# One plan orders all engines of a fused chunk-selecting attention and squared-relu feed-forward

## The chip, the core and the metric

The kernel runs on 1 core of a Trainium2 chip: TensorE (PE, with its weight loads as PEld), VectorE (DVE), ScalarE (ACT), GpSimd (POOL) and SyncE (SP), each with a queue of its own that it works off in order, joined by semaphores. The metric is the device time of one execution in microseconds.

## The reference

```python
def _attn_ref(q, k, v):                  # B, H, S, D = 4, 8, 768, 64
    chunk, nc, top_k, scale = 32, S // 32, 6, 1.0 / np.sqrt(D)
    k_chunks = k.reshape(B, H, nc, chunk, D)
    k_min, k_max = np.min(k_chunks, axis=3), np.max(k_chunks, axis=3)
    ub = np.sum(np.maximum(q[:, :, :, None, :] * k_min[:, :, None, :, :],
                           q[:, :, :, None, :] * k_max[:, :, None, :, :]), axis=-1)
    causal = pos[:, None] // chunk >= np.arange(nc)[None, :]
    ub = np.where(causal, ub, -1000000000.0)
    top_chunks = np.argsort(ub, axis=-1)[..., -top_k:]
    scores = scale * np.matmul(q, k.transpose(0, 1, 3, 2))
    mask = sel & (pos[:, None] >= pos[None, :])      # sel: the key's chunk is in top_chunks
    attn = softmax(np.where(mask, scores, -1000000000.0))
    return np.matmul(attn, v)

x = attn_out.transpose(0, 2, 1, 3).reshape(B * S, H * D)     # 3072 x 512
h = np.maximum(x @ w_in, 0.0)                                # w_in 512 x 2048
out = h * h @ w_out                                          # w_out 2048 x 512
```

## The kernel before

All matmuls are in bfloat16. A batch has 8 heads, taken as 4 pairs, so there are 16 pairs (`p`). A head's 768 positions are 6 tiles of 128. In the first tile of a batch every allowed chunk is among the six best, so it needs no selection: the first tiles of all batches are done ahead (`first_transpose`, `first_scores`, `first_values`), and the other 5 tiles pair by pair.

`stage_a(p)` prepares a pair: it turns the keys on PE (`kT`) and copies them to `kqs` for each head (ACT for p < 3, else DVE), reduces each chunk to its maximum and minimum (`kr`, then `kbds`), turns the queries (`qT`), splits them into positive and negative part (`qp`, `qm`) and copies them to `qss` (ACT), forms the bounds `ub` on PE, masks them (`ubm`), takes each row's 8 largest (`m8`), marks the chunks below the sixth (`selb`), turns these marks on PE (`sT`) and copies them into the last 24 rows of `qss` (DVE). The matching 24 rows of `kqs` hold -32768 for the key's chunk, so that the scores' matmul itself masks what is not selected.

`stage_b(p)` works on 5 banks of 512 score columns for each of 2 heads (`BANKS`): two matmuls into a PSUM bank `ps`, an exp on ACT into `e`, a mask of the diagonal blocks (`causal`: a product with `tri` on DVE for p < 6, an affine select on POOL after that), and four value matmuls of 65 columns into `av`, whose last column is the sum. `normalise` divides on DVE into `x`.

The feed-forward (`ffn_units`) runs on the first tiles of all batches (512 rows, `x_first`) and then on each batch's other 640 rows: `turn` transposes x, `up` makes 128 hidden units for 512 or 320 rows (4 matmuls into `ph`, relu on ACT into `ht`, square on DVE into `h2`), `down` sums 16 hidden blocks into 128 rows of output in four parts, copies them on ACT and stores them from SP's queue.

The order: what PE does in the main part is written by hand. `run_ffn()` lets feed-forward units of the batch before into `stage_b` at a steady rate, after every masked bank; `values` runs `LAG` = 3 banks behind the scores; `beside()` runs one of the four pieces of the next pair's `stage_a` at the banks in `PIECES`; `KEEP` units are left for the end of a batch. The other engines are ordered by the framework's scheduler in that part; in the part of the first tiles all engines go in written order. Loads are issued from POOL's queue in the order of the text: first tiles of k, q, v of batches 0 and 1, then of 2 and 3, w_in's first quarter, then pair by pair the rest of batch 0 with the weights' other quarters between, then batches 1 to 3 tile by tile. POOL must also make the masks, and at most 8 of its loads are under way.

PSUM's 8 banks are `tp` 1 (turned keys and queries), `ps` 3 (scores, also `ub` and `sT`), `av` 2, `ff` 2 (feed-forward); the last batch's `up` uses `ps`.

```python
    with tc.manual_schedule(engines={nc.tensor.engine}):
        ffn.extend(ffn_units(x_first, [S * b for b in range(B)], [(0, 512)]))
...
        run(B)
        aside.append((0, stage_a(0)))
        for n in (2, 2, 2, 2):
            beside()
            run(n)
```

Of the kernel before, what the change touches and what calls it, by code (L numbers as in the profile page):

```python
# [9 lines left out]
F32 = mybir.dt.float32  # L10
# [4 lines left out]
PSUM = bass.MemoryType.PSUM  # L15


@with_exitstack
def kernel(
# [30 lines left out]
    LAG = 3  # L50
# [6 lines left out]
    epool = ctx.enter_context(tc.tile_pool(name="epool", bufs=LAG + 3))  # L57
# [6 lines left out]


    first = {nm: consts.tile([128, B, H, D], BF16, tag=nm + "0", name=nm + "0")
             for nm in "kq"}
    vfirst = consts.tile([128, B, H, VW], BF16, tag="v0", name="v0")
    SRC = {"k": k, "q": q, "v": v}
    nat = {}  # L70

    def load_first(nm, b0, b1):
        dst = vfirst[:, b0:b1, :, 0:D] if nm == "v" else first[nm][:, b0:b1]
        nc.gpsimd.dma_start(
            out=dst.rearrange("p b h d -> p (b h) d"),
            in_=SRC[nm][b0:b1, :, 0:128].rearrange("b h p d -> p (b h) d"))

    def rest(nm, b):
        if (nm, b) not in nat:
            nat[nm, b] = ld.tile([128, NS, H, VW if nm == "v" else D], BF16,  # L80
                                 tag=nm + "n", name=nm + "n")
            if nm == "v":
                nc.gpsimd.memset(
                    nat[nm, b][:, :, :, D:D + 1].rearrange(
                        "p j h o -> p (j h) o"), 1.0)
        return nat[nm, b]

    def load_tile(nm, b, j):
        nc.gpsimd.dma_start(
            out=rest(nm, b)[:, j - 1, :, 0:D],  # L90
            in_=SRC[nm][b, :, 128 * j:128 * (j + 1)].rearrange("h p d -> p h d"))

    def load_pair(nm, b, hp):
        for h in (2 * hp, 2 * hp + 1):
            nc.gpsimd.dma_start(  # L95
                out=rest(nm, b)[:, :, h, 0:D],
                in_=SRC[nm][b, h, 128:].rearrange("(j p) d -> p j d", p=128))

    def key_tile(nm, b, hp, j):
        t = first[nm][:, b] if j == 0 else nat[nm, b][:, j - 1]  # L100
        return t[:, 2 * hp:2 * hp + 2].rearrange("p h d -> p (h d)")

    def value_tile(b, h, j):
        t = vfirst[:, b] if j == 0 else nat["v", b][:, j - 1]
        return t[:, h, 0:D + 1]

    w_in_sb = consts.tile([128, NKI, d_ff], BF16, tag="w_in_sb")
    w_out_sb = consts.tile([128, NFI, d_model], BF16, tag="w_out_sb")

    def load_w_in(f0, f1):  # L110
        cols = slice(128 * f0, 128 * f1)
        nc.gpsimd.dma_start(
            out=w_in_sb[:, :, cols],
            in_=moe_w_in[:, cols].rearrange("(ki p) f -> p ki f", p=128))

    def load_w_out(f0, f1):
        nc.gpsimd.dma_start(
            out=w_out_sb[:, f0:f1],
            in_=moe_w_out[128 * f0:128 * f1].rearrange("(fi p) d -> p fi d", p=128))

    load_first("k", 0, 2)
    ident = consts.tile([128, 128], BF16, tag="ident")
    make_identity(nc, ident)
    load_first("q", 0, 2)
    load_first("v", 0, 2)
    load_first("k", 2, 4)
    load_first("q", 2, 4)
    load_first("v", 2, 4)
    load_w_in(0, 4)
    tri = consts.tile([128, 128], BF16, tag="tri")  # L130
    nc.gpsimd.memset(tri, 1.0)
    nc.gpsimd.affine_select(
        out=tri, in_=tri, compare_op=ALU.is_ge, fill=0.0, base=0,
        channel_multiplier=-1, pattern=[[1, 128]])


# [24 lines left out]
    for i in range(2 * NSET):  # L161
        kq_rows(i)
# [371 lines left out]
```

## Time and profile before

| | |
|---|---|
| time, median of 2 runs | 295.37 us (295.32 to 295.42) |
| profiled execution: its own time | 295.43 us |
| its span, first to last instruction | 293.70 us |
| granted TensorE clock, mean | 0.999 |
| busy PE, PEld | 264.5 us (90%), 172.5 us (59%) |
| busy DVE, ACT, POOL | 190.7 (65%), 195.4 (67%), 102.8 us (35%) |
| DMA, moved in all | 20.61 MB |

The times of the rows are microseconds from the start of the span. Busy time is the union of the recorded spans of an engine's instructions; matmuls overlap, and their recorded ends are modelled. An idle time in brackets names what ended it.

### The profile page before, as it was taken

The page shows a single profiled execution, that of the slowest core. Times are in us where ns is not written, and L with a number is a line of the kernel's source. Part 1 is how long each engine was busy: PE and PEld are TensorE (multiplying, and loading weights), DVE is VectorE, ACT ScalarE, POOL GpSimd, SP SyncE. Part 2 cuts the span into 40 slices and gives each one's busy share as a digit, 9 for nine tenths or more (in the row PEclk, how much of TensorE's full clock was granted, in tenths as well). Part 3 has the DMA queues.
Part 4 walks back from the last instruction along what each step waited for, and adds up shares of the span by engine and source line. Part 5 has one row for each costly group of instructions (what it writes and reads, how often), then busy time and mean ns, then how long its engine had stood idle before and what let it go on. Part 6 is the DMA issues. An engine that isn't in the chain of part 4 may idle for free.

```text
span 293.7 us, 6676 instructions
## 1 busy us (share of the span) xinstructions
PE 264.5 (90%) x2528; PEld 172.5 (59%) x2528; DVE 190.7 (65%) x645; ACT 195.4 (67%) x376; POOL 102.8 (35%) x180
## 2 busy tenths in 40 slices
PE   0578878799899989999998999999989999899994
PEld 0365345565567767555676766557767655577442
DVE  0486777988888989574887895658878720465100
ACT  2223599968768898675788885748798755188211
POOL 8978993999961002121121222111111211000000
PEclk9999999999999999999999999999999999999999
DMA  9999999999999000111100001110000011100011
GB/s 66 168 187 171 160 175 189 155 156 179 175 181 91 1 2 1 38 38 71 38 1 2 3 0 38 71 38 37 2 4 0 2 71 39 71 2 0 36 74 71
DMA packets 82893, 20.61 MB, mean 70 GB/s; under 512 B 75525, under 2 KB 79789, under 8 KB 82861
## 3 DMA queue, kind: packets, MB, share of 16 engines
q0 software_dynamic: 79152, 13.64, 59.6%
q1 hardware_dynamic: 3708, 6.55, 6.0%
q8 instruction: 20, 0.33, 0.4%
q14 instruction: 13, 0.10, 0.1%
HBM read 27.26 MB, written 6.29 MB: 114 GB/s over the span
## 4 chain that ended last, share of the span: by engine, by line
PE 63%; DVE 12%; POOL 8%; ACT 8%; DMA 5%; issue 2%; ACTq 0%; POOLq 0%
PE py L357 25%; PE ph L342 20%; PE ps L427 8%; DVE kr L261 5%; PE av L410 5%; DMA vn<-in_v_dram 3%; ACT ht L347 3%; DVE kqc L258 3%; ACT qsc L281 2%; DMA w_out_sb<-in_moe_w_out_dram 2%; POOL qn L95 2%; POOL kn L95 2%; ACT e L434 2%; PE sT L305 2%; DVE h L350 1%
## 5 line engine op out<-in xcount | busy, mean ns | idle before, releaser
L434 ACT ACTIVATE e<-ps 128x512 bf16<-128x512 f32 x160 | 93.9, 598 | 32.2 <-PE ps L427 29.9
L342 PE MATMUL ph<-xT,w_in_sb 128*128 128x320 bf16 (+1 forms) x576 | 97.8, 312 | 3.0 <-ACT ht L347 2.8
L357 PE MATMUL py<-w_out_sb,h 128*128 128x512 bf16 x384 | 94.7, 378 | 0.0
L347 ACT ACTIVATE ht<-ph 128x320 bf16<-128x320 f32 (+1 forms) x144 | 64.9, 455 | 18.4 <-PE ph L342 10.9
L342 PEld LDWEIGHTS <-w_in_sb 128*128 128x128 bf16 x576 | 56.2, 98 | 29.9 <-issue 7.6
L192 POOL TENSOR_SCALAR_AFFINE_SELECT e<-e 128x128 bf16<-128x128 bf16 x80 | 26.9, 336 | 131.4 <-ACT e L434 131.4
L427 PE MATMUL ps<-qsc,kqc 88*128 88x128 bf16 (+1 forms) x320 | 60.6, 272 | 0.2 <-DVE qsc L309 0.2
L350 DVE TENSOR_TENSOR h<-ht 128x320 bf16<-128x320 bf16 (+1 forms) x144 | 47.0, 333 | 19.2 <-ACT ht L347 18.5
L357 PEld LDWEIGHTS <-h 128*128 128x128 bf16 x384 | 36.9, 97 | 32.5
L410 PEld LDWEIGHTS <-e 128*128 128x128 bf16 x640 | 40.8, 98 | 24.1
L410 PE MATMUL av<-vn,e 128*128 128x65 bf16 x480 | 40.6, 193 | 0.0
L261 DVE TENSOR_REDUCE kr<-kT 128x24 bf16<-128x768 bf16 x32 | 29.2, 953 | 4.5 <-ACT kqc L256 4.4
L362 ACT COPY ob<-py 128x512 f32<-128x512 f32 x24 | 14.1, 586 | 24.2 <-PE py L357 24.1
L281 ACT COPY qsc<-qT 64x640 bf16<-64x640 bf16 x32 | 22.0, 687 | 1.1 <-DVE qm L279 0.5
L427 PEld LDWEIGHTS <-kqc 88*128 88x128 bf16 x320 | 21.7, 98 | 0.8 <-issue 0.2
L258 DVE COPY kqc<-kT 64x768 bf16<-64x768 bf16 x26 | 14.4, 554 | 10.6 <-PE kT L251 10.2
L200 DVE TENSOR_TENSOR x<-av,rc 128x320 bf16<-128x320 f32 (+1 forms) x40 | 19.0, 475 | 0.8
L309 DVE COPY qsc<-sT 24x640 bf16<-24x640 bf16 x32 | 15.5, 483 | 4.9 <-PE sT L305 4.0
L199 DVE RECIPROCAL rc<-av 128x5 f32<-128x5 f32 (+1 forms) x40 | 7.5, 187 | 16.7 <-PE av L410 16.7
L189 DVE TENSOR_TENSOR e<-e,tri 128x128 bf16<-128x128 bf16 (+2 forms) x56 | 14.4, 258 | 3.6 <-ACT e L434 2.0
L296 DVE MAX8 m<-ubm 128x8 f32<-128x24 f32 x160 | 15.4, 172 | 0.5
L410 PE MATMUL av<-v,e 128*128 128x65 bf16 x160 | 15.4, 194 | 0.0
(61 smaller groups left out, 234.4 us busy)
## 6 DMA issues: line engine op xcount, KB each, us to landing
out_dram<-ob SPq DMA_DIRECT2D x24, 256.0 KB, 2.7
w_in_sb<-in_moe_w_in_dram POOLq DMA_DIRECT2D x4, 512.0 KB, 8.0
w_out_sb<-in_moe_w_out_dram POOLq DMA_DIRECT2D x4, 512.0 KB, 8.6
kn<-in_k_dram POOLq DMA_DIRECT2D x15, 128.0 KB, 6.7
qn<-in_q_dram POOLq DMA_DIRECT2D x15, 128.0 KB, 6.8
vn<-in_v_dram POOLq DMA_DIRECT2D x15, 128.0 KB, 6.3
kn<-in_k_dram POOLq DMA_DIRECT2D x8, 80.0 KB, 5.9
qn<-in_q_dram POOLq DMA_DIRECT2D x8, 80.0 KB, 5.2
```

The costliest lines, as they stand in the source:

```text
L192: nc.gpsimd.affine_select(out=e, in_=e, compare_op=ALU.is_ge, fill=0.0, base=0, channel_multiplier=-1, pattern=[[0, n], [1, 128]])
L200: nc.vector.tensor_mul(x, av[:, :, 0:D], rc[:, 0:n].unsqueeze(2).to_broadcast([128, n, D]))
L258: nc.vector.tensor_copy(kqs[0:D, s, hh], pt[D * hh:D * hh + D])
L261: nc.vector.tensor_reduce(kr[:, mm], pt.rearrange("d (c j) -> d c j", j=CH), axis=AX.X, op=op)
L281: nc.scalar.copy(qss[0:D, s, hh], pt[D * hh:D * hh + D])
L342: nc.tensor.matmul(ph, lhsT=w_in_sb[:, ki, 128 * f:128 * (f + 1)], rhs=xT[:, ki, c0:c1], start=(ki == 0), stop=(ki == NKI - 1))
L347: nc.scalar.activation(ht, ph, ACT.Relu)
L350: nc.vector.tensor_mul(h2[f][:, c0:c1], ht, ht)
L357: nc.tensor.matmul(py, lhsT=h2[f][:, 128 * t:128 * (t + 1)], rhs=w_out_sb[:, f, :], start=(f == 0), stop=(f == NFI - 1))
L410: nc.tensor.matmul(av[:, t - 1], lhsT=e[:, 128 * c:128 * (c + 1)], rhs=value_tile(b, 2 * hp + hh, j), start=(i == 0 and c == 0), stop=(i = ...
L427: nc.tensor.matmul(ps[:, 128 * c:128 * (c + nt)], lhsT=kqs[:, s, hh, 128 * j:128 * (j + 1)], rhs=qss[:, s, hh, 128 * (t0 - 1):128 * (t0 - ...
L434: nc.scalar.activation(e, ps, ACT.Exp, scale=scale)
```

## The change

A class `Plan` takes every step of the kernel as an operation: the engines that may do it with a rough duration in us for each, a due time in half steps (20 to a pair, a pair's preparation due 30 earlier), the operations that it needs, the buffers that it uses, and for a load the packets. `order()` simulates the engines: it always takes the operation that can start first, and among those of the same engine that can start within 0.06 us the one due first. Loads keep their listed order, 8 under way at most; buffers come free when the last user is done, plus a hand-over; reads of one PSUM tile by two engines don't overlap; PE's durations are doubled up to 14 us. The operations are then written out in the order of their planned starts, and all engines run in that order.

Other things that go with it: key copies, query copies, selection copies, x copies, relus and output copies go to DVE or ACT, diagonal masks to DVE or POOL, whichever the plan finds free. The first tiles' causal mask is added on PE (a product of `ident` with `ahead`, 512 columns for each of 8 banks) instead of multiplied on DVE. `sT` is turned in 3 matmuls (two tiles each) instead of 5 and copied in 4 pieces instead of 2. The keys and queries of the first tiles are turned into separate banks. Loads: w_in's first quarter and pair 0's k and q come before the first tiles of batches 2 and 3. Eight matmuls of 512 columns on a constant run at the very start. The first quarter of the first feed-forward's ups runs in two halves of 256 columns.

```diff
--- before.py
+++ after.py
+    HAND_OVER = {"PE": 0.22, "ACT": 0.10, "DVE": 0.10, "POOL": 0.12, "SP": 0.1}
+    BUSY = 0.06
+    WAIT = 0.06
+    WARM = 14.0
+    NEVER = 1e9
...
+        while ready:
+            found = []
+            for op in ready:
+                if op.packets and op is not self.loads[len(landed)]:
+                    continue
+                at = 0.0
+                new = {}
+                for t in op.tiles:
+                    if not t.held:
+                        new[t.tag] = new.get(t.tag, 0) + 1
+                for tag, n in new.items():
+                    at = max(at, sorted(slots[tag])[n - 1]
+                             if n <= len(slots[tag]) else self.NEVER)
+                if at == self.NEVER:
+                    continue
+                if op.packets and len(landed) >= 8:
+                    at = max(at, landed[-8])
+                for engine, cost in op.where.items():
+                    st = max(at, free[engine])
+                    for n in op.needs:
+                        same = n.engine == engine and not n.packets
+                        lag = (0.0 if engine == "PE" else self.BUSY) if same                             else self.HAND_OVER[n.engine]
+                        st = max(st, n.end + lag)
+                    for t in op.tiles:
+                        if t.psum:
+                            for e, end in t.last.items():
+                                if e != engine and "PE" not in (e, engine):
+                                    st = max(st, end + self.HAND_OVER[e])
+                    found.append((st, op, engine, cost))
+            assert found, "nothing can start"
+            first = min(found, key=lambda f: f[0])
+            st, op, engine, cost = min(
+                (f for f in found if f[2] == first[2] and f[0] <= first[0] + self.WAIT),
+                key=lambda f: (f[1].due, f[0]))
+            ready.remove(op)
+            if engine == "PE" and st < self.WARM:
+                cost *= 2
+            op.engine, op.start, op.end = engine, st, st + cost
+            free[engine] = op.end
+            if op.packets:
+                queue = max(queue, op.end + 1.3) + op.packets * 0.00098
+                op.end = queue + 0.35
+                landed.append(op.end)
+            for t in op.tiles:
+                if not t.held:
+                    t.held = True
+                    slots[t.tag].remove(min(slots[t.tag]))
+                t.last[engine] = max(t.last.get(engine, 0.0), op.end)
+                t.left -= 1
+                if not t.left:
+                    slots[t.tag].append(
+                        max(u.end + self.HAND_OVER[u.engine] for u in t.users))
+            for n in waiting.get(op, ()):
+                count[n] -= 1
+                if not count[n]:
+                    ready.append(n)
+            done.append(op)
...
+    def write(self):
+        for op in self.order():
+            for t in op.tiles:
+                if t.tile is None:
+                    t.tile = t.make()
+            op.fn(op.engine)
...
+    plan = Plan({"tp": 1, "ps": 3, "av": 2, "ff": 2, "e": 6, "h2": NFI + 6, "ht": 3,
+                 "ob": 3, "kn": B - 1, "qn": B - 1, "vn": B - 1, "x": 2, "xT": 2,
+                 "kr": 2, "qp": 2, "qm": 2, "ubm": 2, "m8": 2, "rc": 2})
...
+    load_first("k", 0, -998)
+    made["ident"] = plan.op({"POOL": 0.75}, -997, lambda _: make_identity(nc, ident))
+    load_first("q", 0, -996)
+    load_first("v", 0, -995)
+    made["ahead"] = plan.op({"POOL": 0.55}, -994, make_ahead)
+    made["tri"] = plan.op({"DVE": 0.15}, -900, lambda _: nc.vector.tensor_single_scalar(
+        tri, ahead, 0.0, op=ALU.is_ge), [made["ahead"]])
+    made["rows", 0] = plan.op({"ACT": 0.84}, -999, lambda _: kq_rows(0),
+                              [made["ident"]])
+    for i in range(1, 2 * NSET):
+        made["rows", i] = plan.op({"SP": 0.8}, -999 + i, lambda _, i=i: kq_rows(i),
+                                  [made["rows", 0]])
+
+    load_w_in(0, 4, -990)
+    made["ubmask"] = plan.op({"POOL": 1.45}, -971, make_ubmask)
+    ones(0, -980)
+    load_pair("k", 0, 0, -989)
+    load_pair("q", 0, 0, -988)
+    for nm in "kqv":
+        load_first(nm, 2, -987)
+    load_w_in(4, 8, -986)
+    load_pair("v", 0, 0, -985)
...
+                load_tile(nm, b, j, 20 * NP * b - 70 + 5 * i + j)
...
+    made["warm"] = plan.op({"PE": 1.7}, -999, lambda _: warm_up(8), [made["vector"]])
...
+            for hh in range(2):
+                nc.tensor.matmul(ps[hh].tile, lhsT=ident,
+                                 rhs=ahead.unsqueeze(1).to_broadcast(
+                                     [128, NP, 128]),
+                                 start=True, stop=False, skip_group_check=True)
...
+        t0 = HALVES * p - LEAD
+        before = scored.get(p - NSET, [])
...
+        def turn_selection(_):
+            for i in range(0, NT, 2):
+                transpose(sT[:, i // 2], selbs[:, s, i:i + 2])
...
+        kc = [op({"DVE": 0.50, "ACT": 0.75}, t0 + 3 + hh + late, lambda e, hh=hh: copy(
+            e, kqs[0:D, s, hh], kT[D * hh:D * hh + D]),
+            [t] + before, [kT]) for hh in range(2)]
...
+    HALVES = 20
+    LEAD = 30
...
-    PIECES = (0, 3, 5, 8)
-    KEEP = 4
...
+                sc = plan.op({"PE": 0.225}, due, scores, prepared[p, hh], [ps])
+                scored[p].append(sc)
+                done = plan.op({"ACT": 0.54}, due + 0.5, lambda _, e=e, ps=ps:
+                               nc.scalar.activation(e.tile, ps.tile, ACT.Exp,
+                                                    scale=scale), [sc], [ps, e])
                 if diagonal:
                     d0, d1 = diagonal
-                    causal(e[:, 128 * d0:128 * d1].rearrange(
-                        "p (n j) -> p n j", j=128), d1 - d0, p < 6)
-                run_ffn()
-                behind.append(lambda p=p, hh=hh, i=i, e=e, x=x:
-                              values(p, hh, i, e, x))
-                if len(behind) > LAG:
-                    behind.pop(0)()
-                if len(BANKS) * hh + i in PIECES:
-                    beside()
-
-
+                    n = d1 - d0
+                    done = plan.op(
+                        {"DVE": 0.10 + 0.07 * n, "POOL": 0.2 + 0.13 * n}, due + 1.5,
+                        lambda en, e=e, d0=d0, d1=d1: causal(
+                            en, e[:, 128 * d0:128 * d1].rearrange(
+                                "p (n j) -> p n j", j=128), d1 - d0),
+                        [done, made["tri"]], [e])
+                prev = plan.op({"PE": 0.125}, due + 5, values,
+                               [done, prev, made["ones", b]] + loads_of("v", b, hp),
+                               [e, av, nat["v", b]])
...
+            op = plan.op({"ACT": 0.06 + w / 960, "DVE": 0.06 + w / 960}, at[0] + 0.5,
+                         relu, [op], [ph, ht])
+            squared.setdefault(f, []).append((c0, c1, plan.op(
+                {"DVE": 0.02 + w / 1200}, at[0] + 2, lambda _: nc.vector.tensor_mul(
+                    h2[f][:, c0:c1], ht.tile, ht.tile), [op], [ht, h2[f]])))
...
+            op = plan.op({"ACT": 0.54, "DVE": 0.53}, at[0] + 1,
+                         lambda e: copy(e, ob.tile, py.tile), [op], [py, ob])
...
+        turn, up, down = ffn(
+            x, lambda t, b=b: x_done[b, 1], [S * b + 128 * t for t in range(1, NT)],
+            None, HALVES * NP * (b + 1) + 10, 2.2, ("ps", "ps") if last else ("ff", "ff"))
...
+        plan.write()
```

## Rows read from the trace of the kernel before

**Rows 1.** Groups by shape, whole run: line, engine, tiles, shapes, count | busy us, mean ns | idle.

```profile
L357 PE MATMUL py<-w_out_sb,h 128*128 128x512 bf16 x384 | 94.7, 378 | 0.0
...
L342 PE MATMUL ph<-xT,w_in_sb 128*128 128x320 bf16 x512 | 79.9, 298 | 3.0 <-ACT ht L347 2.8
...
L347 ACT ACTIVATE ht<-ph 128x320 bf16<-128x320 f32 x128 | 55.4, 437 | 13.2 <-PE ph L342 6.1 <-DVE h L350 1.0 <-PE ps L427 0.3
L427 PE MATMUL ps<-qsc,kqc 88*128 88x384 bf16 x128 | 41.3, 323 | 0.0
...
L410 PE MATMUL av<-vn,e 128*128 128x65 bf16 x480 | 40.6, 193 | 0.0
...
L342 PE MATMUL ph<-xT,w_in_sb 128*128 128x512 bf16 x64 | 17.9, 418 | 0.0
L200 DVE TENSOR_TENSOR x<-av,rc 128x320 bf16<-128x320 f32 x32 | 15.6, 488 | 0.5
L309 DVE COPY qsc<-sT 24x640 bf16<-24x640 bf16 x32 | 15.5, 483 | 4.9 <-PE sT L305 4.0
```

**Rows 2.** The chain that ended last, at its end: start us, us, what.

```profile
255.25 17.52 PE ph L342 x128
272.77 17.28 PE py L357 x80
```

**Rows 3.** Windows: length, each engine's busy us (instructions), granted clock, DMA share, GB/s.

```profile
0.00:26.00 26.00, 13.28 (x120) 9.60 (x121) 12.45 (x39) 6.71 (x11) 21.62 (x35) 1.00 1.71 143
0.00:37.00 37.00, 22.90 (x171) 13.98 (x172) 20.19 (x65) 13.18 (x21) 32.27 (x48) 1.00 1.73 151
37.00:90.00 53.00, 46.62 (x518) 30.52 (x517) 44.31 (x157) 42.94 (x75) 43.65 (x53) 1.00 2.06 172
90.00:254.00 164.00, 159.25 (x1626) 107.12 (x1625) 114.27 (x388) 122.36 (x244) 26.86 (x80) 1.00 0.10 26
254.00:290.00 36.00, 35.71 (x221) 20.86 (x218) 11.93 (x36) 16.34 (x36) 0.00 (x0) 1.00 0.10 37
```

The engines stand in the order PE, PEld, DVE, ACT, POOL.

**Rows 4.** Timeline of PE, 6 to 38 us: start, us, what, [idle before].

```profile
6.12 0.61 PE L213 MATMUL T<-ident,k 128*128 128x128 bf16 x4 [6.12 <-DMA k<-in_k_dram]
...
24.77 0.74 PE L251 MATMUL kT<-ident,kn 128*128 128x128 bf16 x5
25.39 3.57 PE L342 MATMUL ph<-xT,w_in_sb 128*128 128x512 bf16 x8
...
31.71 1.89 PE L342 MATMUL ph<-xT,w_in_sb 128*128 128x512 bf16 x8
...
37.00 0.38 PE L427 MATMUL ps<-qsc,kqc 88*128 88x256 bf16 x2
```

**Rows 5.** Timeline of POOL's queue, 16 to 85 us.

```profile
16.96 0.86 POOL L95 DMA_DIRECT2D vn<-in_v_dram  x1 [0.34 <-DMA v<-in_v_dram]
...
19.49 1.73 POOL L95 DMA_DIRECT2D kn<-in_k_dram  x2 [1.67 <-DMA w_in_sb<-in_moe_w_in_dram]
...
51.99 1.75 POOL L89 DMA_DIRECT2D qn<-in_q_dram  x2 [1.66 <-DMA w_out_sb<-in_moe_w_out_dram]
...
84.14 0.27 POOL L83 MEMSET vn<- 128x40 bf16 x1 [2.32 <-PE av L410]
```

**Rows 6.** Waits, whole run: engine and line, released by: us, times, longest us.

```profile
PE sT L305 <- DVE selb L297: 3.1, 5, 1.4
...
PE ph L342 <- ACT ht L347: 2.8, 5, 0.9
```

**Rows 7.** Groups by shape, 37 to 90 us, of DVE and of ACT.

```profile
L189 DVE TENSOR_TENSOR e<-e,tri 128x128 bf16<-128x128 bf16 x28 | 6.0, 215 | 2.0 <-ACT e L434 1.8
...
L281 ACT COPY qsc<-qT 64x640 bf16<-64x640 bf16 x10 | 6.9, 687 | 0.3 <-DVE qm L279 0.2
```

**Rows 8.** Line L350, 255 to 290 us and 90 to 254 us: ns min/median/max, first and last start.

```profile
L350 DVE TENSOR_TENSOR h<-ht x32: 324/326/326, 256.3 to 273.3; 128x320 bf16<-128x320 bf16 x32
...
L350 DVE TENSOR_TENSOR h<-ht x95: 278/321/542, 91.3 to 230.6; 128x320 bf16<-128x320 bf16 x95
```

More of the change, by code (lines that the diff above doesn't have):

```diff
@@ L15, with __init__, __getitem__ @@
 PSUM = bass.MemoryType.PSUM
+class Buffer:
+    def __init__(self, tag, make, psum=False):
+        self.tag, self.make, self.psum = tag, make, psum
+        self.users = []
+        self.left = 0
+        self.tile = None
+        self.held = False
+        self.last = {}
+    def __getitem__(self, key):
+        return self.tile[key]
+class Op:
+    def __init__(self, where, due, fn, needs, tiles, packets):
+        self.where, self.due, self.fn = where, due, fn
+        self.needs, self.tiles, self.packets = needs, tiles, packets
+        self.engine = None
+        self.start = self.end = None
@@ L78, in rest @@
[L78 to L119, printed above, removed]
@@ L130, with transpose @@
+    def transpose(dst, src):
+        nc.tensor.matmul(dst, lhsT=src, rhs=ident, is_transpose=True,
+                         start=True, stop=True)
+    ident = consts.tile([128, 128], BF16, tag="ident")
+    ahead = consts.tile([128, 128], BF16, tag="ahead")
     tri = consts.tile([128, 128], BF16, tag="tri")
[L131 to L134, printed above, removed]
+    warm = consts.tile([128, 128], BF16, tag="warm")
@@ L234, in first_values, with load @@
-    def first_values(b):
-        es = e_first.pop(b)
-        for hh in range(2):
-            av = psav.tile([128, NP, D + 1], F32, tag="av", name="av0")
+    made = {}
+    made["vector"] = plan.op({"DVE": 1.1}, -999, vector_constants)
+    SRC = {"k": k, "q": q, "v": v}
+    nat = {}
+    loaded = {}
+    order = []
+    def load(key, fn, due, packets, tiles=(), cost=0.88):
+        op = plan.op({"POOL": cost}, due, fn, tiles=tiles, packets=packets)
+        loaded.setdefault(key, []).append(op)
@@ new lines, in ones, with go, load_tile @@
+    def ones(b, due):
+        def go(engine):
+            e = nc.vector if engine == "DVE" else nc.gpsimd
+            e.memset(nat["v", b].tile[:, :, :, D:D + 1].rearrange(
+                "p j h o -> p (j h) o"), 1.0)
+        made["ones", b] = plan.op({"DVE": 0.12, "POOL": 0.3}, due, go,
+                                  tiles=[nat["v", b]])
+    def load_tile(nm, b, j, due):
+        load((nm, b), lambda _: nc.gpsimd.dma_start(
+            out=nat[nm, b].tile[:, j - 1, :, 0:D],
+            in_=SRC[nm][b, :, 128 * j:128 * (j + 1)].rearrange("h p d -> p h d")),
+            due, 1024, [nat[nm, b]])
@@ new lines, with warm_up, first_transposes, turn @@
+    t_first = {}
+    x_done = {}
+    def warm_up(n):
+        wt = psav.tile([128, 4, 128], F32, tag="av", name="wt")
+        for _ in range(n):
+            nc.tensor.matmul(wt, lhsT=warm,
+                             rhs=warm.unsqueeze(1).to_broadcast([128, 4, 128]),
+                             start=True, stop=True)
+    made["warm"] = plan.op({"PE": 1.7}, -999, lambda _: warm_up(8), [made["vector"]])
+    def first_transposes(nm, b, tag, due):
+        pt = buffer(tag, [128, NP, 128], name="T0")
+        t = t_first[nm, b] = buffer("h2", [128, NP, 128], name="t0")
+        def turn(_):
+            for hp in range(NP):
+                transpose(pt[:, hp], key_tile(nm, b, hp, 0))
+        op = plan.op({"PE": 0.23}, due, turn,
+                     loaded[nm, b, "first"] + [made["ident"]], [pt])
+        t.op = plan.op({"DVE": 0.36, "ACT": 0.53}, due + 0.5,
+                       lambda e: copy(e, t.tile, pt.tile), [op], [pt, t])
```

664 lines of the change are left out of this document (373 added, 291 removed).

## The prediction

> **What bounds the kernel now.** I first read the counts by shape of the whole run, to know how much streaming TensorE cannot avoid, and then the windows, to see where it did not stream. The page's busy time of PE (264.5 us, 90%) is no measure of it: a matmul of 65 columns shows 193 ns and one of 512 shows 378 [rows 1], and these overlap. What one costs in a row of others is read from the tail, where nothing else runs: 128 matmuls of 320 columns in 17.52 us, 137 ns each, and 80 of 512 in 17.28 us, 216 ns each [rows 2]. That is 0.42 ns a column; for the other widths I put about 2.5 ns on top (128 columns 56 ns, 384 162 ns, and as estimates at the same pace 30 ns for 65 columns and 26 ns for 48).
>
> With the counts [rows 1]: down 384 x 0.216 = 82.9; up 512 x 0.137 + 64 x 0.216 = 84.0; scores, 160 banks of 512 columns in two pieces each (128 of them as 384 + 128, in the row, 32 as 256 + 256) x 0.218 = 34.9; values 640 x 0.030 = 19.2 (480 in the row, 160 read the first tiles); 416 transposes and small scores of 128 columns x 0.056 = 23.3; 192 short ones 5. Together about 248.5 us of streaming, in a span of 293.7. TensorE bounds the kernel, and 45.2 us are lost to it.
>
> The same prices, counted inside each window [rows 3], say where. Up to 26 only 6.2 us are streamed, up to 37 it is 13.6: lost 23.4. From 37 to 90, 43.9: lost 9.1. From 90 to 254, 155.8: lost 8.2. From 254 to 290, 35.2: lost 0.8. After the last matmul (272.77 + 17.28 = 290.05 [rows 2]) 3.65 remain for the last copy and store. These make the 45.2. So the places to look at are the first 37 us and then the attention of batch 0, up to about 85; the long steady part streams 95% of its time.
>
> The start is bound by arrivals and by the written order. The first keys land at 6.12, yet the keys of pair 0 are turned at 24.77 and its first scores run at 37.00 [rows 4]. Its data were there sooner: v of batches 2 and 3, sixth in the queue, lands by 16.96, w_in's first quarter by 19.49, as the waits of the POOL queue show [rows 5]; pair 0's keys are next, about 20.8. Then they wait because run(B) is written ahead of stage_a(0): the turns of x_first of all four batches come first on PE. Also to be seen there: eight matmuls of 512 columns take 3.57 us at 25.39 (446 ns each, half pace) and 1.89 at 31.71 (full pace) [rows 4], while the granted clock reads 1.00, the 2.4 GHz level, all along [rows 3]. The pace tells more here than that column.
>
> From 37 to 90 DVE is busy 44.3 and ACT 42.9 of 53 us [rows 3], and PE waits for single steps made there (sT for selb 3.1, an up for the relu before it 2.8 [rows 6]). The last values of batch 0 end about 84, when POOL may fill the next vn [rows 5].
>
> **The change, part by part.** *Loads and start.* Three of the six first loads (batches 2 and 3) move behind w_in's first quarter and pair 0's k and q. Five such loads landed between 6.12 and 16.96 [rows 4, 5], 2.17 us each, so three fewer bring pair 0's data 6.5 us sooner: keys at 14.3, queries about 15.7. No matmul of batches 2 and 3 stands before the turn any more. From the turn to the scores it took 37.00 - 24.77 = 12.2 us [rows 4] with relus and squares between; I take 11.5, and scores start at 26. What waits behind the moved loads is batches 2 and 3 (about 21.5 for 17) and w_in's second quarter, some 2 us later; their matmuls can fill after 26. By 26 are streamed: first attention 4.5, a quarter of the first ups 3.5, pair 0's turns; some 8 us. Lost by 26: 18, where the kernel now loses 23.4 by its first scores. Bounds: 16 if the preparation takes 9.5 us, and 22 if its 12.2 us stay, the half pace lasts as long as now and DVE is held by batches 2 and 3. The eight warming matmuls lie before 6.12 beside the first load, at nothing; without that cover they would be 8 x 0.446 = 3.6 us. If they keep the full pace up, they save up to 8 x (0.446 - 0.236) = 1.7 us on the first ups; I count none.
>
> *Attention of batch 0 beside the first feed-forward.* Masks may go to POOL (the 28 single ones are 6.0 us of DVE in the window [rows 7]). Relus and the copies of x, out, keys and queries may go to DVE or ACT (query copies alone are 6.9 us of ACT [rows 7]). DVE and ACT do 87.2 of 106 us; without those masks 81.2, evenly spread 40.6 of 53 each. POOL is busy for 43.7 of the 53 [rows 3], so not all masks move. Both come off the edge, and what they do not hold, TensorE can stream if data are there: w_out's quarters land until 52 (the POOL queue's last wait for them ends there [rows 5]), and the new order asks for the same bytes before them. I give half of the 9.1 back: lost 4.5, between 2 and 9.1. Costs without a row: a relu on DVE lies between 0.24 (half of a 640-column copy from PSUM, 0.483) and 0.488 (the 320-column product from PSUM), against 0.437 on ACT [rows 1]; it is nearest to the upper one, so the swap costs nothing but evens the load. Four selection copies in place of two cost between the same 1.0 us a pair and 2.0, on engines with that much to spare.
>
> *Fewer and more matmuls.* Three turns of sT for five: 16 x 2 x 0.056 = -1.8. The first masks as eight 512-column products: 8 x 0.216 = +1.7, and eight wide DVE masks go. Streaming stays at 248.4.
>
> *The steady part.* ACT, DVE, POOL and SP now also run in the plan's order, each instruction behind all earlier ones of its engine; before, in this part, only PE's was written by hand. A relu or copy that the plan puts too early holds the exps queued behind it, they the values, and those PE. On the other side pair preparation starts 30 half steps ahead (one and a half pairs), so the turns should not meet an unfinished step. No row shows that order, so its cost is bounded: 2 us lost if nearly every stop goes, 8.2 as now, and the slower rival beyond. DVE works 114 and ACT 122 of 164 us there [rows 3], so neither is late on the whole. I take 5, between the two.
>
> A rule speaks against masks on POOL. The squares took 324 to 326 ns in the tail, without POOL, and 278 to 542 beside its masks, with the median at 321 [rows 8]. The Trainium skill, "SBUF — State Buffer", section "Who interferes with whom", says that a DVE instruction with two SBUF inputs contends with a GpSimd instruction that reads SBUF, and that the second to issue fully blocks. The 542 agrees, the median says that it is seldom. Were each of the 136 masks to block DVE for that 0.22 us, it would be 30 us of its time in 230; by the median it is nothing, and that I take.
>
> *The tail.* Same matmuls, same last copy and store: 0.8 + 3.65.
>
> **Sum.** 248.4 + 18 + 4.5 + 5 + 0.8 + 3.65 = 280.4 us of span. The profiled execution took 295.43 with a span of 293.70, so 1.73 lie outside it, and it is 0.06 above the median. The time is 282 (-4.5%). With the low ends (16, 2, 2) it is 275, with the high ends (22, 9.1, 8.2) 294.
>
> **Rivals.** *The gain is given back in batch 0* (20%). Pair 0 starts early, but POOL, busy 82% there with issues, takes few masks, DVE stays as full, and four pairs take the 47 us from 37.00 to 84 [rows 4, 5] again. They would end at 73, but with 52 us of streaming at hand until then at most, and PE waits for what DVE and ACT owe. The loss after 26 then stays at 9.1 or grows by up to 5 of the 5.4 won: 248.4 + 18 + 9.1 to 14 + 8.2 + 4.45 + 1.73 = 290 to 295; I put it at 292. For it: no load lands sooner after w_out. Against: 82% is not full.
>
> *Head-of-line blocking* (12%, slower). The rough durations put instructions of ACT, DVE and POOL in an order that the real ones do not follow. The place is POOL, then ACT, in each pair: a mask stands behind a DMA issue that waits, as one did for 1.66 us [rows 5], its values behind it, and with six e buffers the exps stop. My sum has 13.4 us to lose, so it decides from 0.84 us a pair over 16 pairs; at 1.4 a pair, most of such a wait, it is 282 + 22 = 304. For it: POOL's share of issues. Against: they end by 90, and after that POOL did 27 us in 164 [rows 3].
>
> *The plan fits nearly everywhere* (13%): the low ends, 275 and a little less if the warm start also counts. For it: the slack of DVE and ACT after 90. Against: all four queues must keep step.
>
> **How the numbers follow.** The forecast, 282, has 55% with its own range of 276 to 289. A measurement of this kernel tells about 2% (5.9 us) from no change, so faster means below 289.5: the forecast's 55%, the fitting plan's 13% and 4% of the first rival's. Within 2% are the other 16% of that and a mild blocking, 2%. Slower keeps 10%. For 8 in 10 the range runs from 273 to 293: the bounds of the sum, and half of the first rival.
>
> **What would show it.** Right, if the first key turns of pair 0 run near 15 and its scores near 26, if batch 0's last values end near 70 to 74, if relus stand on both engines and some masks on POOL before 70, and if the counted loss after 90 is nearer to 5 than to 8. Wrong, if the scores still start after 32 (the start's term), if PE waits for relus, masks or selb more than the 2.8 and 3.1 us of now (the plan's order), or if streaming itself is not 248.

## The result and the profile after

The changed kernel takes 284.78 us (284.24 to 285.32, 2 runs) against 295.37: a ratio of 0.964, 95% interval 0.956 to 0.972. The forecast was 282, its range 273 to 293. The profiled execution took 285.32 with a span of 283.6.

I count what is streamed and lost as before. The trace of the changed kernel lacks 27 matmul records, 25 of `down` and 2 of `up` (their weight loads are all there: 384 and 592); they are put back at their pace, 216 ns each, 5.8 us, in the windows where those weight loads stand. The eight warming matmuls don't count. Streamed: 248.4 us.

| lost to TensorE, us | 0 to 37 | 37 to 70 | 70 to 90 | 90 to 254 | 254 to the end |
|---|---|---|---|---|---|
| before | 23.4 | 6.7 | 2.3 | 8.2 | 4.5 |
| changed | 20.0 | 0.5 | 6.9 | 3.7 | 4.1 |

Windows of the changed kernel (columns as in [rows 3]):

```profile
0.00:37.00 37.00, 27.31 (x213) 15.90 (x215) 21.06 (x73) 18.19 (x33) 31.91 (x46) 0.82 1.71 153
37.00:70.00 33.00, 32.59 (x342) 20.48 (x347) 29.70 (x101) 26.55 (x49) 28.91 (x44) 1.00 1.95 179
70.00:76.00 6.00, 4.92 (x70) 3.32 (x69) 5.78 (x23) 5.54 (x11) 5.73 (x10) 1.00 1.82 153
76.00:83.00 7.00, 6.15 (x62) 5.02 (x62) 6.21 (x24) 5.50 (x12) 5.73 (x9) 0.51 2.07 132
83.00:90.00 7.00, 6.29 (x85) 4.75 (x82) 6.54 (x17) 6.58 (x15) 6.58 (x11) 1.00 1.73 111
90.00:254.00 164.00, 162.33 (x1602) 110.43 (x1615) 129.53 (x434) 118.39 (x230) 25.99 (x70) 1.00 0.16 31
```

Of the 10 us, 3.4 came up to 37, only 1.6 from 37 to 90, and 4.5, the largest part, from the steady part after 90. From 37 to 70 TensorE hardly stops, then it loses 6.9 us in 20: most of what the first stretch won was lost again in the second. In 70 to 76 DVE is busy 5.78 of 6 us and ACT 5.54, and right after that the granted clock is 0.51, the 1.2 GHz level, up to about 83.

Timeline of PE in the changed kernel's start (answers to [rows 4]):

```profile
14.55 0.30 PE L217 MATMUL kT<-ident,k 128*128 128x128 bf16 x1
15.53 0.69 PE L217 MATMUL kT<-ident,kn 128*128 128x128 bf16 x5 [0.69 <-DMA kn<-in_k_dram]
...
19.05 1.87 PE L681 MATMUL ph<-xT,w_in_sb 128*128 128x256 bf16 x8 [0.18 <-DVE xT L214]
...
29.89 1.05 PE L681 MATMUL ph<-xT,w_in_sb 128*128 128x256 bf16 x8 [0.52 <-DVE xT L214]
30.78 0.38 PE L601 MATMUL ps<-qsc,kqc 88*128 88x256 bf16 x2
```

and of DVE, between the turn and the scores of pair 0:

```profile
16.26 0.96 DVE L525 TENSOR_REDUCE kr<-kT 128x24 bf16<-128x768 bf16 x1 [0.85 <-PE kT L217]
17.14 0.17 DVE L461 RECIPROCAL rc<-av 128x4 f32<-128x4 f32 x1
...
18.48 0.42 DVE L214 COPY xT<-xt 128x512 bf16<-128x512 bf16 x1 [0.25 <-PE xt L217]
...
20.10 0.42 DVE L690 TENSOR_SCALAR ht<-ph 128x256 bf16<-128x256 f32 x1 [0.41 <-PE ph L681]
...
21.94 0.94 DVE L525 TENSOR_REDUCE kr<-kT 128x24 bf16<-128x768 bf16 x1
...
26.09 0.42 DVE L463 TENSOR_TENSOR x<-av,rc 128x256 bf16<-128x256 f32 x1
```

The turn of pair 0's loaded keys (`kn`) came 9 us sooner (15.53, before 24.77 [rows 4]; worked out was 14.3), but from it to the scores it took 15.3 us, not 11.5. The second reduction starts only at 21.94, behind x, copies, a relu and squares of the first tiles, and from 25.9 to 28.9 the four divisions into x of batches 2 and 3 (one is shown) stand between the steps that choose the chunks.

Two moments from the timelines of ACT and POOL, the last output of the first feed-forward and the last values of batch 0 (84.14 before [rows 5]). In the kernel before, the first feed-forward's last `down` ran at 84.08 (timeline of PE, shown first):

```profile
84.08 1.03 PE L357 MATMUL py<-w_out_sb,h 128*128 128x512 bf16 x4
```

```profile
71.77 0.58 ACT L212 COPY ob<-py 128x512 f32<-128x512 f32 x1
```

```profile
79.05 0.27 POOL L306 MEMSET vn<- 128x40 bf16 x1 [0.84 <-PE av L612]
```

So between 72 and 79 TensorE had only attention to do: up to 76 at the pace of DVE and ACT, and from 76 on at the 1.2 GHz level too. Batch 0's four pairs took 48.2 us from their first scores (30.78) to their last values, as long as the 47.0 before; 37 to 90 has DVE busy 48.2 and ACT 44.2 of 53 us, more than the 44.3 and 42.9 of before [rows 3]. Groups of the page that answer to the free choice of engine (mask on POOL, relu on ACT, relu on DVE, mask on DVE):

```profile
L581 POOL TENSOR_SCALAR_AFFINE_SELECT e<-e 128x128 bf16<-128x128 bf16 (+1 forms) x88 | 29.8, 340 | 122.8 <-ACT e L623 122.3
...
L688 ACT ACTIVATE ht<-ph 128x320 bf16<-128x320 f32 (+2 forms) x82 | 37.0, 451 | 21.7 <-PE ph L681 18.7
...
L690 DVE TENSOR_SCALAR ht<-ph 128x320 bf16<-128x320 f32 (+2 forms) x66 | 32.6, 495 | 7.4 <-PE ph L681 4.6
...
L578 DVE TENSOR_TENSOR e<-e,tri 128x128 bf16<-128x128 bf16 (+1 forms) x40 | 9.2, 233 | 9.6 <-ACT e L623 9.1
```

### The profile page after: what moved, and what is told of

It reads as the page before. It is cut to its first block, busy times and chain, and to the rows that moved or that the text cites. A ratio compares the mean times of both kernels' runs of the same rounds, so it can differ in the third digit from the quotient of the medians.

```text
span 283.6 us, 6676 instructions
## 1 busy us (share of the span) xinstructions
PE 265.4 (94%) x2501; PEld 173.8 (61%) x2528; DVE 207.2 (73%) x695; ACT 187.8 (66%) x359; POOL 104.8 (37%) x185
## 4 chain that ended last, share of the span: by engine, by line
PE 81%; DVE 9%; DMA 3%; POOL 2%; ACT 2%; issue 2%; POOLq 0%; ACTq 0%; DVEq 0%
PE ph L681 29%; PE py L711 27%; PE ps L601 11%; PE av L612 6%; DMA kn<-in_k_dram 3%; PE xt L217 2%; PE kT L217 2%; DVE kr L525 2%; PE qT L217 2%; DVE x L463 1%; DVE m L505 1%; DVE qsc L214 1%; PE sT L217 1%; PE ub L497 1%; PE ub L499 1%
## 5 line engine op out<-in xcount | busy, mean ns | idle before, releaser
L681 PE MATMUL ph<-xT,w_in_sb 128*128 128x320 bf16 (+2 forms) x590 | 97.5, 305 | 1.5 <-DVE xT L214 0.7
L711 PE MATMUL py<-w_out_sb,h 128*128 128x512 bf16 x359 | 89.9, 379 | 1.2
L581 POOL TENSOR_SCALAR_AFFINE_SELECT e<-e 128x128 bf16<-128x128 bf16 (+1 forms) x88 | 29.8, 340 | 122.8 <-ACT e L623 122.3
L688 ACT ACTIVATE ht<-ph 128x320 bf16<-128x320 f32 (+2 forms) x82 | 37.0, 451 | 21.7 <-PE ph L681 18.7
L699 DVE TENSOR_TENSOR h<-ht 128x320 bf16<-128x320 bf16 (+2 forms) x148 | 46.0, 331 | 3.1 <-ACT ht L688 1.5
L690 DVE TENSOR_SCALAR ht<-ph 128x320 bf16<-128x320 f32 (+2 forms) x66 | 32.6, 495 | 7.4 <-PE ph L681 4.6
L212 ACT COPY kqc<-kT 64x768 bf16<-64x768 bf16 x23 | 18.2, 793 | 1.6 <-PE kT L217 1.3
L578 DVE TENSOR_TENSOR e<-e,tri 128x128 bf16<-128x128 bf16 (+1 forms) x40 | 9.2, 233 | 9.6 <-ACT e L623 9.1
L612 PE MATMUL av<-v,e 128*128 128x65 bf16 x160 | 15.3, 195 | 0.0
L212 ACT COPY qsc<-sT 24x384 bf16<-24x384 bf16 (+1 forms) x32 | 13.4, 418 | 1.7 <-PE sT L217 0.7
L313 POOL DMA_DIRECT2D qn<-in_q_dram x15 | 13.4, 900 | 0.3 <-DMA w_out_sb<-in_moe_w_out_dram 0.3
```

The costliest lines, as they stand in the source:

```text
L212: nc.scalar.copy(dst, src)
L581: nc.gpsimd.affine_select(out=e, in_=e, compare_op=ALU.is_ge, fill=0.0, base=0, channel_multiplier=-1, pattern=[[0, n], [1, 128]])
L612: nc.tensor.matmul(av[:, t - 1], lhsT=e[:, 128 * c:128 * (c + 1)], rhs=value_tile(b, h, j), start=(i == 0 and c == 0), stop=(i == len(BANK ...
L681: nc.tensor.matmul(ph.tile, lhsT=w_in_sb[:, ki, 128 * f:128 * (f + 1)], rhs=xT[:, ki, c0:c1], start=(ki == 0), stop=(ki == NKI - 1))
L688: nc.scalar.activation(ht.tile, ph.tile, ACT.Relu)
L690: nc.vector.tensor_scalar_max(ht.tile, ph.tile, 0.0)
```

## The experiments

The kernel before was run again beside each group of four; ratios are to those runs. The losses come from one profiled execution of each run, whose time lies up to 1.4 us from the median and whose clock fell and rose at its own times, so a difference of 1 us between two rows is no finding. The changed kernel was run only twice, and its interval is the widest.

| run | us | ratio to before, 95% | lost 0 to 37 | 37 to 70 | 70 to 90 | 90 to 254 |
|---|---|---|---|---|---|---|
| changed kernel | 284.78 | 0.964 (0.956 to 0.972) | 20.0 | 0.5 | 6.9 | 3.7 |
| e1_spread | 281.56 | 0.956 (0.952 to 0.961) | 19.5 | 1.7 | 1.6 | 3.9 |
| e2_fixed | 290.23 | 0.984 (0.982 to 0.987) | 19.2 | 0.7 | 10.0 | 6.2 |
| e8_fixed_spread | 286.54 | 0.972 (0.969 to 0.976) | 21.2 | 1.9 | 5.0 | 5.8 |
| e10_relu_act | 283.59 | 0.963 (0.960 to 0.965) | 19.6 | 1.6 | 4.3 | 4.8 |
| e7_pe_only | 305.19 | 1.036 (1.033 to 1.038) | 24.1 | 4.9 | 7.3 | 14.1 |
| e3_old_loads | 283.61 | 0.964 (0.960 to 0.968) | 16.8 | 1.4 | 5.3 | 4.0 |
| e4_no_warm | 284.93 | 0.965 (0.961 to 0.969) | 19.1 | 0.5 | 6.3 | 3.9 |
| e5_before_start | 297.75 | 1.010 (1.007 to 1.014) | 26.1 | 6.2 | 2.8 | 7.5 |
| e9_before_halves | 304.12 | 1.032 (1.029 to 1.035) | 23.5 | 8.7 | 3.2 | 12.8 |
| e6_best | 278.20 | 0.943 (0.941 to 0.946) | 16.0 | 3.0 | 2.6 | 2.8 |
| e12_whole_ups | 279.49 | 0.952 (0.945 to 0.959) | 16.5 | 2.5 | 2.9 | 3.5 |
| e13_mask_dve | 279.21 | 0.948 (0.945 to 0.951) | 17.6 | 3.1 | 3.3 | 2.9 |

**e1_spread: the filler lasts longer.**

```diff
     turn, up, down = ffn(x_first, lambda t: x_done[t, 0], first_rows, None,
-                         -60, 4.7)
+                         -60, 6.2)
```

> Only the first feed-forward's due rate changes, 4.7 to 6.2 half steps for each us of PE work, so that its units last until batch 0's attention ends. Theory (filler): the 7 us lost between 70 and 90 in the changed kernel come from the first feed-forward being used up by 72 while DVE and ACT are full with pairs 3 and 4; spread, the loss in 70 to 85 falls from 6 to about 2, the clock is not halved there, and the time falls by 2 to 4 us to about 281 to 283. Rival (DVE and ACT bound): the pairs take what they take, the loss only moves to before 70, and the time stays within 1 us of 284.8.

Measured 281.56. Its windows over the same stretch:

```profile
70.00:76.00 6.00, 6.00 (x69) 3.73 (x69) 5.54 (x14) 5.41 (x11) 5.21 (x9) 1.00 2.10 171
76.00:83.00 7.00, 6.29 (x81) 4.51 (x78) 6.75 (x24) 6.25 (x13) 6.86 (x12) 1.00 1.55 101
```

The loss falls from 6.9 to 1.6 and the clock stays at the 2.4 GHz level, with DVE and ACT about as full as in the changed kernel. The filler theory holds; only 1.2 us moved ahead of 70 (0.5 to 1.7). One thing isn't parted: in 76 to 83 the changed kernel streamed 3.3 us' worth at half pace, so a part of its 3.7 lost there is the clock's. In e3, with the filler as it was, the clock stayed at the 2.4 GHz level from 70 to 90 and 5.3 us were lost, so the clock is the smaller part.

**e2_fixed, e8_fixed_spread, e10_relu_act: one engine for each step.** e2 takes the choice away from each copy, relu and mask (the diff shows two of the eight places), e8 also spreads the filler, e10 takes only the relus' choice.

```diff
...
-            op = plan.op({"ACT": 0.06 + w / 960, "DVE": 0.06 + w / 960}, at[0] + 0.5,
+            op = plan.op({"ACT": 0.06 + w / 960}, at[0] + 0.5,
...
-                        {"DVE": 0.10 + 0.07 * n, "POOL": 0.2 + 0.13 * n}, due + 1.5,
+                        {"DVE": 0.10 + 0.07 * n} if p < 6 else {"POOL": 0.2 + 0.13 * n}, due + 1.5,
...
```

> The plan stays, but each copy, relu and mask has the one engine it had before the change (relus, output and query copies on ACT, x and selection copies on DVE, key copies on ACT for p < 3 and else DVE, masks on DVE for p < 6 and else POOL). Theory (free choice of engine gives the part up to 90): the pairs of batch 0 slow down to the 10 us of before, 4 to 6 us are lost again up to 90 and under 2 after it, time 290 to 292. Rival (order alone does it): time within 1.5 us of 284.8.

> Fixed engines as in the run with fixed engines, and the first feed-forward spread (6.2 instead of 4.7). It tells whether free engines save time by themselves or only by making the pairs quick enough for the filler to last. Theory (DVE and ACT bound batch 0, free choice shortens the pairs): spreading gives little here, 1 to 2 us, time 288.5 to 289.5, as the pairs still take 10 us. Rival (pace of the filler is all): it falls as far as with free engines, by 3 us or more, to 285 to 287.

> The changed kernel with all relus on ACT; every other step keeps its choice of engine. Theory (relus are most of what free choice moves: 66 of 148 went to DVE): half or more of the 5.4 us by which fixed engines were slower, time 287.5 to 289.5. Rival (masks and copies are what counts): within 1.5 us of 284.8.

Free choice is worth 5.4 us with the filler as it was (290.23 to 284.78) and 5.0 with it spread (286.54 to 281.56); spreading is worth 3.7 with fixed engines and 3.2 with free ones. The two add up: my expectation for e8, that spreading would give 1 to 2 us there, was wrong. The rival had the time right (286.54, within 285 to 287), but not its reason, that the filler's pace is all: with the filler spread, free choice still is worth 5.0. The place was not as expected either. From 37 to 70 fixed engines lose no more (0.7) than free ones; they lose 3 us more from 70 to 90 and 2.5 more after 90. Batch 0's four pairs take 52.1 us with fixed engines, from 30.04 to the last values at 82.1, behind which POOL fills the next vn, against 48.2:

```profile
30.04 0.38 PE L601 MATMUL ps<-qsc,kqc 88*128 88x256 bf16 x2
```

```profile
L306 POOL MEMSET vn<- x1: 268/268/268, 82.2 to 82.2; 128x40 bf16 x1
```

In e2, ACT has slack in just the stretch where PE loses most; in the changed kernel it is busy 5.50 there:

```profile
76.00:83.00 7.00, 5.19 (x49) 3.77 (x50) 5.98 (x18) 3.56 (x6) 4.17 (x7) 0.66 2.43 156
```

The relus' choice isn't needed for it: with all 148 on ACT the time is 283.59, no slower. The choice of copies and masks is enough; these I didn't part further, and no run gives the relus alone their choice.

**e7_pe_only: PE in the plan's order, the other engines in the framework's.**

```diff
-    with tc.manual_schedule():
+    with tc.manual_schedule(engines={nc.tensor.engine}):
         plan.write()
```

> The plan is written out as in the changed kernel, with the same engine for each step, but only PE runs in the written order; ACT, DVE, POOL and SP are ordered by the framework's scheduler, as in the main part of the kernel before. Theory (one order for all queues matters): the framework's order puts late steps first here and there, 2 to 6 us more, time 287 to 291, most of it up to 90 where DVE and ACT are full. Rival (PE's order and the engine choice are all): within 1.5 us of 284.8.

It lost far more than the theory said, 20 us, half of it after 90 (14.1 for 3.7), where DVE and ACT have slack:

```profile
90.00:254.00 164.00, 157.34 (x1604) 107.01 (x1604) 129.54 (x443) 122.08 (x238) 28.03 (x76) 0.99 0.12 25
```

Every step stands on the same engine as in the changed kernel, and PE's order is the same. PE now works off an order that the other engines don't keep. Its longest wait by the whole run is for values behind a mask (0.2 in the changed kernel, 5.4 now); after 90 it is for a relu (3.1, where the changed kernel has none). These and the smaller waits are some 6 of the 10 us lost after 90; the rest has no row.

```profile
PE av L612 <- POOL e L581: 5.4, 4, 2.3
PE ph L681 <- ACT ht L688: 3.1, 6, 1.1
```

**e3_old_loads, e5_before_start, e9_before_halves: the start.** e3 puts all loads of the start back in their old order inside the plan (the change also had w_in's third and fourth quarter and w_out's first ahead of the next pair's k and q):

```diff
+    for nm in "kqv":
+        load_first(nm, 2, -991)
     load_w_in(0, 4, -990)
...
-    load_pair("k", 0, 0, -989)
-    load_pair("q", 0, 0, -988)
-    for nm in "kqv":
-        load_first(nm, 2, -987)
...
```

> The plan stays, but the loads stand in the order of the kernel before (first tiles of batches 2 and 3 ahead of w_in's first quarter and pair 0). Theory of the prediction (load order brings pair 0 forward): pair 0's key turns move from 14.5 to about 20.5 and its first scores by as much, 3 to 5 us are lost again, time 288 to 290. Rival (the written order of PE was what held pair 0, and early matmuls of batches 2 and 3 fill the time): time within 1.5 us of 284.8.

e5 makes the new loads and an early pair 0 in the kernel before, without a plan:

```diff
+    load_w_in(0, 4)
+    load_pair("k", 0, 0)
+    load_pair("q", 0, 0)
     load_first("k", 2, 4)
...
+        aside.append((0, stage_a(0)))
+        beside()
+        beside()
+        first_transpose(2)
+        first_transpose(3)
+        beside()
...
         run(B)
...
+        beside()
+        run(8)
...
```

> The kernel before with its start alone changed: w_in's first quarter and pair 0's k and q load before the first tiles of batches 2 and 3, and PE's written order has pair 0's key and query turns and its bounds ahead of the first attention of batches 2 and 3 and of the turns of x_first. No plan. Theory (the start is 3 to 5 us of the gain by itself): first scores of pair 0 move from 37 to 28 to 31, time 290 to 292.5. Rival (without the plan the filler is missing then, or DVE is late): within 1.5 us of 295.4.

e9 gives the kernel before early half ups instead:

```diff
...
+        run(2)
+        first_transpose(2)
+        first_transpose(3)
+        run(4)
+        first_scores(2)
...
         aside.append((0, stage_a(0)))
-        for n in (2, 2, 2, 2):
+        beside()
+        run(2)
+        run(4)
+        for n in (2, 2, 2):
```

> The kernel before with one part alone: the first feed-forward's turns and four half ups of batches 0 and 1 stand in PE's written order ahead of the scores of batches 2 and 3; pair 0 starts behind their values and ahead of the other turns. Same loads, no plan. Theory (the written order of the start is worth some 3 us without any plan): loss up to 37 falls from 23.4 to about 20, time 291 to 293. Rival (the filler is then missing later, as DVE and ACT set the pace of the pairs up to 87): within 1.5 us of 294.8.

PE's timeline in e3, pair 0's turn and its scores:

```profile
20.94 0.44 PE L217 MATMUL kT<-ident,kn 128*128 128x128 bf16 x5
...
36.90 0.38 PE L596 MATMUL ps<-qsc,kqc 88*128 88x256 bf16 x2
```

The scores are back at 36.90, as in the kernel before [rows 4], and the time is 283.61: no slower than the changed kernel, with 3.2 us less lost up to 37 and batch 0's last values at 75.5 for 79.0. The theory that the load order earns the start is refuted. That the old order is the better one is not shown: the ratios are the same, and in its profile the clock rose for good at 14.9, in the changed kernel's at 21.4, between which the latter streamed 2.7 us' worth at half pace. In the kernel before, neither move helps. e5 lost 26.1 up to 37, though pair 0's keys were turned at 15.29; its scores ran only at 39.7, behind eight ups (31.91 to 39.68) that its written order puts ahead of them, so it is no clean test of early scores. e9 lost 23.5 and more in every later stretch; PE's waits for a relu rise from 2.8 to 5.6, and what in the other engines' order causes that stays open.

**e4_no_warm: without the eight matmuls at the start.**

```diff
-    made["warm"] = plan.op({"PE": 1.7}, -999, lambda _: warm_up(8), [made["vector"]])
```

> Without the eight warming matmuls at the start. In the changed kernel the granted clock is back at half from 7.9 to 21.3, so the theory is that they buy nothing: time within 1 us of 284.8, half pace up to 21 to 30. Rival (they bring the full pace sooner than the kernel before has it): full pace only near 29, 2 to 4 us more.

284.93 in the median of four (three of 284.04 to 285.81, one of 289.22): they buy nothing.

**e6_best and two steps off it.** e6 joins e3 with a spread filler and lets the later feed-forwards run on later due times (2.4 for 2.2), which was not tried alone:

```diff
...
-                         -60, 4.7)
+                         -50, 5.2)
...
-            None, HALVES * NP * (b + 1) + 10, 2.2, ("ps", "ps") if last else ("ff", "ff"))
+            None, HALVES * NP * (b + 1) + 10, 2.4, ("ps", "ps") if last else ("ff", "ff"))
```

> The plan with the load order of the kernel before, and the first feed-forward spread by its due times (from -50 at 5.2 half steps a us, before -60 at 4.7), the later ones at 2.4 instead of 2.2. Theory (the filler's pace is the one thing still lost up to 90, and the load order costs nothing): start as in the plan with old loads, loss from 70 to 90 about 2, time 279 to 281.5, below both kernels. Rival (old loads help only because they use the filler earlier, spreading takes that back): 282 to 284.

278.20, better than both kernels: 5.7% under the kernel before, and below the expected range. The windows 0 to 37 and 90 to 254:

```profile
0.00:37.00 37.00, 28.60 (x255) 16.38 (x256) 22.55 (x80) 21.89 (x39) 32.60 (x47) 1.00 1.74 151
...
90.00:254.00 164.00, 163.26 (x1597) 110.20 (x1594) 131.21 (x438) 114.80 (x229) 22.90 (x63) 1.00 0.15 31
```

e12 turns all first tiles before any up, with no halves (the first two lines); e13 masks the first tiles on DVE again (the rest):

```diff
-    for f in range(4):
-        up(f, 0, 256, f)
...
-                nc.tensor.matmul(ps[hh].tile, lhsT=ident,
-                                 rhs=ahead.unsqueeze(1).to_broadcast(
...
+            e = plan.op({"DVE": 0.38}, due + 0.4, lambda _, hh=hh: nc.vector.tensor_mul(
+                es[hh].tile, es[hh].tile,
...
```

> The best version so far (plan, old load order, spread filler), but the first feed-forward's first quarter isn't cut in halves of 256 columns: all four turns come first, then ups of 512. Theory (the halves let PE stream before batches 2 and 3 are there): the loss up to 26 grows by the 1.8 us that four halves stream, time 279.5 to 281 against 278.2. Rival (other work fills, or the time is won back before 90): within 1 us of 278.2.

> The best version, with the first tiles' causal mask as a product on DVE behind the exp again, in place of the eight 512-column products on PE. 1.7 us of streaming go, about 3.4 us of DVE come and one more hand-over in each first tile's chain. Theory (DVE is what is short up to 90): 279 to 281. Rival (PE is): 276 to 277.5.

Each step back costs about 1 us (279.49 and 279.21 against 278.20), hardly clear of the noise: the intervals of both overlap e6's. e13 streams 1.7 us less and loses 1.6 more up to 37. That fits DVE being dearer than PE there, but in e13's profile the 1.2 GHz level lasted to 21.2 and in e6's the pace was full from 12.5, so it isn't shown.

## Why the prediction was right, and where its steps failed

The direction and the size came as forecast, 284.78 for 282; the place did not. The sum cut the start at 26, where it put the first scores. In these stretches, before, forecast and measured:

| | before | forecast | measured |
|---|---|---|---|
| streaming | 248.5 | 248.4 | 248.4 |
| lost up to 26 | 19.8 | 18 | 17.4 |
| lost from 26 to 90 | 12.7 | 4.5 | 10.0 |
| lost from 90 to 254 | 8.2 | 5 | 3.7 |
| lost after that | 4.5 | 4.45 | 4.1 |

The forecast had 10.0 of its 13.2 us before 90; measured are 5.1 of 10.1. The stretch from 26 to 90 was mis-sized by 5.5 us, beyond its upper bound of 9.1, and that the sum is only 3 us low is in part luck: the other terms were 2.3 too dear. (The prediction's terms of streaming, as printed, add up to 249.3; the same count by unrounded prices is 248.4.) Two steps are behind the 5.5.

*Loads and start: the scores at 26 failed.* They ran at 30.78, and 2.7 us were lost from 26 to 37. The data did come sooner: with the old loads inside the plan (e3) the turn runs at 20.94, with the new ones at 15.53, and the rest of the 9 us is the plan's order. But the 11.5 us of preparation was mis-sized (15.3). DVE was held by the first tiles of batches 0 and 1, their half ups, and then batches 2 and 3; the last I had put into the upper bound alone. And the mechanism behind it was wrong: early scores of pair 0 earn nothing by themselves, because what counts is that TensorE has something to stream. In e3, with scores at 36.90, the time is the same and 16.8 us are lost up to 37 for 20.0. What the start did gain is not had by PE's order alone, the plan's (e7) or one of mine (e5, e9): 23.5 to 26.1 us were lost up to 37 with ACT, DVE and POOL in another order. Nor does it need the free choice of engine (e2, 19.2). That the full pace comes sooner, near 21 instead of 30, goes with it; how much of the start is due to that was not parted.

*Attention of batch 0: not freed where I said.* The loss from 37 to 70 went to nearly nothing, but with fixed engines too (e2, 0.7), so the plan's order did that, which draws the first feed-forward forward: it was streamed by 72, before by 85. Free choice, worth 5 us by e2 and e8, works behind 70. It makes the pairs shorter than the same plan does without it (48.2 for 52.1 us), not shorter than before (47.0), and so batch 0's values ended at 79, not 70 to 74, and TensorE stood beside full engines with its filler gone. That is the first rival's place and mechanism, four pairs in 47 us again; its price of 290 to 295 did not come, as the steady part gave more. e1 and e8 show that the filler's pace alone is 3 to 4 us of it.

*The steady part* came out better than taken, 3.7 for 5, and gave the largest gain. By e2 (6.2) some 2 us of the 4.5 came with fixed engines, the rest with the free choice. The slower rival, head-of-line blocking, is refuted as a net cost: taking the written order away from ACT, DVE and POOL cost 20 us. The waits of PE that I had named, ups for the relu and sT for the marks, went from 2.8 and 3.1 to 0.6 and 0.5 by the waits of the changed kernel:

```profile
PE ph L681 <- ACT ht L688: 0.6, 1, 0.6
...
PE sT L217 <- DVE selb L549: 0.5, 1, 0.5
```

*Small terms.* Relus of 320 columns, by the groups with the shapes kept apart:

```profile
L688 ACT ACTIVATE ht<-ph 128x320 bf16<-128x320 f32 x68 | 29.7, 437 | 16.8 <-PE ph L681 14.3 <-DVE ht L690 1.1 <-ACT e L623 0.4
L690 DVE TENSOR_SCALAR ht<-ph 128x320 bf16<-128x320 f32 x60 | 29.2, 489 | 5.7 <-PE ph L681 3.0
```

DVE's 489 ns is my upper end (488), ACT's is 437; by e10 the swap costs nothing that can be seen. Squares beside POOL's masks and in the tail without them (answers to [rows 8]):

```profile
L699 DVE TENSOR_TENSOR h<-ht x107: 306/318/470, 90.4 to 253.3; 128x320 bf16<-128x320 bf16 x107
```

```profile
L699 DVE TENSOR_TENSOR h<-ht x16: 315/317/319, 256.4 to 264.2; 128x320 bf16<-128x320 bf16 x16
```

Medians 318 and 317. Of the 107, 13 began while a mask ran on POOL; eight of these took 398 to 470, and all others of the 107 took 327 at most, so the masks cost DVE some 0.9 us in all. What the Trainium skill ("SBUF — State Buffer", "Who interferes with whom") says of two SBUF inputs beside POOL shows in these eight. But the worst was held for some 150 ns, with 291 of its mask still to run by the profile, whose spans on POOL are rough: a full block isn't seen. The warming matmuls are worth nothing, as counted. The turns of sT in three matmuls with four copies, and the separate banks of the first tiles, were not tried alone.

## What to carry to other kernels

Where one engine sets the end and others feed it, count what it must stream and find the stretches where it has nothing to stream; an earlier arrival helps only if it fills one of them. Independent work kept for the stretch in which the feeders are full was worth 3 to 4 us here, a free choice of engine for the feeders' steps 5, and both added up. A planned order for the main engine needs the same order on the engines that serve it: on PE alone it took 305.19 us, more than the hand-written order of PE that it replaced (295.37). And a forecast by stretches is to be checked by stretches: here the total was close and the places were not.

## What the runs showed of the hardware

The granted clock can read 1.00 while matmuls run at half pace. In the kernel before it read 1.00 from the start, with 446 ns for 512 columns at 25.39 [rows 3, 4]; the trace's list of levels has its first entry only at 30.2 us, the 2.4 GHz level, and 512 columns took 236 ns at 31.71. In e6 the first entry is at 12.5; the column reads 1.00 from 8 to 14, and eight turns of 128 columns took 1.03 us in it, and 0.62 behind it:

```profile
8.00:14.00 6.00, 4.53 (x44) 2.43 (x44) 1.80 (x6) 2.00 (x4) 5.90 (x8) 1.00 2.31 176
```

```profile
9.44 1.03 PE L217 MATMUL T<-ident,q 128*128 128x128 bf16 x8 [1.60 <-DMA q<-in_q_dram]
...
15.38 0.62 PE L217 MATMUL T<-ident,q 128*128 128x128 bf16 x8 [0.22 <-DMA q<-in_q_dram]
```

So in these traces the column says nothing ahead of the list's first entry, and the pace does. Where there are entries the two agree: in the changed kernel it read 0.50 from 8 to 21, and 256 columns took 234 ns each at 19.05 and 131 at 29.89.

The level also fell in the middle of a kernel: behind 70 to 76, where PE was busy 4.92 of 6 us, it was 0.51 in the mean of the next 7 us, in which PE looked busy (6.15 of 7) and streamed only 3.3 us' worth of columns (e1, at the 2.4 GHz level: 5.8 in the same stretch).
